# One-core decode attention beside a Mish layer: pack-by-pack loops with planned waits become loops over single batches with token semaphores

## The chip, the cores and the metric

The kernel runs on one core of one Trainium2 chip. The metric is the device time of one execution in microseconds (us); the kernel before takes 1303.63 us, the median of three runs (1303.53 to 1303.74). Engines are named as in the profile: PE (TensorE; PEld is its weight load), DVE (VectorE), ACT (ScalarE), POOL (GpSimd) and SP (SyncE, which issues the loads here).

## The reference

```python
xn = _layernorm(x, axis=-1)                                   # x: 8 x 1 x 512
q = (xn @ wq).reshape(8, 1, 32, 128).transpose(0, 2, 1, 3)    # 32 heads of 128
k = jnp.repeat(k_cache, 4, axis=1)                            # 8 kv heads, 8192 keys, 128
v = jnp.repeat(v_cache, 4, axis=1)
scores = jnp.einsum("bhqd,bhkd->bhqk", q, k) * (128 ** -0.5)
o = jnp.einsum("bhqk,bhkd->bhqd", _softmax(scores), v)
attention = o.transpose(0, 2, 1, 3).reshape(8, 1, 4096) @ wo
h = xn @ w1 + b1                                              # 512 -> 1792
mish = (h * jnp.tanh(softplus(h))) @ w2                       # 1792 -> 512
out = x + attention + mish
```

All is float32. The two caches hold 268 MB each; wq and wo 8.4 MB each, w1 and w2 3.67 MB each.

## The kernel before, in words

A **unit** is one batch with a pair of kv heads: 8.39 MB of keys and 8.39 MB of values, each one load of 64 KB per partition. There are 32 units. Two of them (batches 2k and 2k+1 of the same pair of heads) make a **pack**; 16 packs. Four packs make one pair of heads through all eight batches. wq and wo are loaded in four quarters each, one for each pair of heads.

Buffers: kvw holds a quarter of wq or wo; kva holds values; kvb holds keys and is a quarter larger than a unit, so that the next keys may overwrite the first three quarters of the old ones before the last quarter is read (plan_k; the products run forward in one unit and backward in the next).

For each unit, PE multiplies the keys with the queries (scores, tile c). The queries stand in qT, spread by a mask over 64 columns, so a product fills a 128x64 tile of the array, and two such tiles (two column halves) work side by side: 32 products, which PE runs as 64 passes. ACT copies c to sc, and PE sums it by the selection csel into the rows of S (rows, tile s), for both units of a pack.

For each pack, after its second unit: DVE takes the maximum over s, has it turned twice by PE (tiles nm, nr, nx, nmx), and makes the shifts nms (maximum). ACT takes exponents of s in two halves (exponents); DVE transposes each half from wide to raw, folds it, and adds the parts into the weights pt (fold, weights); the sums of the exponents go to l, ls, lsel (row_sums).

For each unit, PE then multiplies the values with pt (values, tile o): 32 products of 128x32 tiles, four side by side, 64 passes. **The values that a pack's loop multiplies are those of the pack before** (p - 1), so their weights are complete long ahead. DVE gathers o by quarters into os (gather), PE merges it (merge), DVE normalises it into oT (collect). After four packs oT is turned into oW (turn) and multiplied with a quarter of wo (outputs); DVE adds the result to acc.

Who waits for whom is worked out ahead of the build: class Program records every operation with the tiles it reads and writes, finds the conflicts, gives every pair of engines a semaphore and writes each wait at its instruction. PE, DVE and ACT run a hardware loop over packs 1 to 15; pack 0 and the end are written out. Each rare part (turn, queries, outputs) sits under a condition. The loads are in one queue on SP, in a planned order (plan, pump, release): each is issued when its buffer is free. With pack p's keys of unit b come the values of unit b of pack p - 1. The end of the queue loads w2 in three parts and the last quarter of wo in two, alternately; small products of w2 and wo then fill PE, after rounds of filler products (unread) that nobody reads.

All instructions of the kernel before carry line 383 (Program.issue) in the profile.

Of the kernel before, what the change touches and what calls it, by code (L numbers as in the profile page):

```python
# [8 lines left out]
AF = mybir.ActivationFunctionType  # L9
ALU = mybir.AluOpType  # L10
AX = mybir.AxisListType

P = 128
B = 8
# [23 lines left out]
PACKS = PAIRS * NP  # L38
R = P // G
# [5 lines left out]


KX = KR // 4

# [11 lines left out]
W2R = G * FT // 2 * FP // P  # L60
FAR = 1e38


ENGINES = ("tensor", "vector", "scalar", "gpsimd", "sync")
LOOPED = ("tensor", "vector", "scalar")
FIRST, END = 1, PACKS
RARE = ("w",)
SOMETIMES = {
    "turn": lambda p: (p + 27) & 19,
    "queries": lambda p: (p + 1) & 19,  # L70
    "outputs": lambda p: (p + 27) & 19,
}


class Op:
    def __init__(self, engine, method, make=None, outs=(), ins=(), stream=None, to=None):
        self.engine, self.method, self.make = engine, method, make
        self.outs, self.ins, self.to = outs, ins, to
        self.who = stream or engine
        self.unit = 16 if stream else 1  # L80
        self.waits = []


class Engine:
    def __init__(self, program, name):
        self.program, self.name = program, name

    def vary(self, method, make):

        args = make(self.program.pack)  # L90
        return self.add(method, args, {}, make)

    def __getattr__(self, method):
        return lambda *args, **kw: self.add(method, args, kw)

    def add(self, method, args, kw, make=None):
        more = {k: kw.pop(k) for k in ("stream", "to") if k in kw}
        after = kw.pop("after", ())
        outs = [kw["out"] if "out" in kw else args[0]]
        outs += [kw["accum_out"]] if "accum_out" in kw else []  # L100
        aps = [a for a in (*args, *kw.values()) if isinstance(a, bass.AP)]
        here = [a for a in aps if a.tensor.name in self.program.on_chip]
        ins = [a for a in here if not any(a is o for o in outs)]
        outs = [a for a in outs if a.tensor.name in self.program.on_chip]
        op = Op(self.name, method, make, outs, ins, **more)
        op.args, op.kw = args, kw
        return self.program.add(op, after)


class Program:  # L110

    def __init__(self, nc):
        self.nc = nc  # L120
        self.ops, self.count = [], {}
        self.know = {e: {} for e in ENGINES}
        self.seen = {}
        self.on_chip, self.psum = set(), set()
        self.pack, self.name, self.zone, self.at = None, None, "before", 0
        self.sends, self.numbers = {}, {}
        self.starts, self.sems, self.unit = {}, {}, {}

    def __getattr__(self, engine):
        if engine not in ENGINES:  # L130
            raise AttributeError(engine)
        return Engine(self, engine)

    def enter(self, pack):
        looped = pack in range(FIRST, END)
        if looped or self.zone == "loop":
            self.starts[pack] = len(self.ops)
        self.zone = "loop" if looped else "after" if self.starts else "before"
        self.pack, self.at, self.name = pack, 0, None

    def part(self, name):

        self.name = name
        self.at += 1

    def relay(self, engine, to, after):

        return self.add(Op(engine, "relay", to=to), [after])

    def settle(self, engine):  # L150

        last = [o for o in self.ops if o.who == engine][-1]
        self.add(Op(engine, "settle"), [last])

    @staticmethod
    def region(ap):
        (step, n), *free = ap.ap
        p, f = divmod(ap.offset, step)
        return p, p + n, f, f + 1 + sum(s * (c - 1) for s, c in free)

    def conflicts(self, op):

        found = {}
        for ap, writes in [(a, False) for a in op.ins] + [(a, True) for a in op.outs]:
            r = self.region(ap)
            for (who, wrote, q), o in self.seen.setdefault(ap.tensor.name, {}).items():
                if who == op.engine == "tensor":
                    continue
                hit = r[0] < q[1] and q[0] < r[1] and r[2] < q[3] and q[2] < r[3]
                hit = hit and (writes or wrote)  # L170
                if ap.tensor.name in self.psum and who != op.engine:
                    hit = all(
                        r[k] // n <= (q[k + 1] - 1) // n and q[k] // n <= (r[k + 1] - 1) // n
                        for k, n in ((0, 32), (2, 512))
                    )
                if hit and (who not in found or o.n > found[who].n):
                    found[who] = o
        return sorted(found.values(), key=lambda o: -len(o.clock))
# [1004 lines left out]
```

## Time and profile before

| | |
|---|---|
| median of the timed runs | 1303.63 us |
| the profiled execution, first to last instruction (its span) | 1302.2 us |
| busy: PE, DVE, ACT | 869.0, 389.9, 122.2 us |
| moved by the load queue | 561.06 MB |
| passes of keys x queries (tile c), without filler | 2048, in 32 units |
| passes of values x weights (tile o) | 2048, in 32 units |

The execution that was profiled took 1302.2 us from its first to its last instruction; the median of the timed runs lies 1.4 us above that. A row of the timeline has the start in us, the busy time in us, the engine, the line, the operation, the tiles as written<-read, shapes and count; in brackets stands the idle time of the engine ahead of it and what ended it. "64*128 64x512" is a product with 64 rows and 128 columns of weights and 512 columns streamed. A row of the waits has the total, the number of times and the longest.

### The profile page before, as it was taken

The page shows a single profiled execution, that of the slowest core. Times are in us where ns is not written, and L with a number is a line of the kernel's source. Part 1 is how long each engine was busy: PE and PEld are TensorE (multiplying, and loading weights), DVE is VectorE, ACT ScalarE, POOL GpSimd, SP SyncE. Part 2 cuts the span into 40 slices and gives each one's busy share as a digit, 9 for nine tenths or more (in the row PEclk, how much of TensorE's full clock was granted, in tenths as well). Part 3 has the DMA queues.
Part 4 walks back from the last instruction along what each step waited for, and adds up shares of the span by engine and source line. Part 5 has one row for each costly group of instructions (what it writes and reads, how often), then busy time and mean ns, then how long its engine had stood idle before and what let it go on. Part 6 is the DMA issues. An engine that isn't in the chain of part 4 may idle for free.

```text
span 1302.2 us, 11363 instructions
## 1 busy us (share of the span) xinstructions
PE 869.0 (67%) x4814; PEld 278.5 (21%) x4814; DVE 389.9 (30%) x597; ACT 122.2 (9%) x294; POOL 4.8 (0%) x10
## 2 busy tenths in 40 slices
PE   4786666766567665686656686666866656756568
PEld 1222112212112221122211222111221121212113
DVE  6350504305051230521405132052320515105061
ACT  1020202001020100200102020020100102001020
POOL 1000000000000000000000000000000000000000
PEclk9898789887799788897877897778877888878779
DMA  9999999999999999999999999999999999999998
GB/s 404 447 419 446 421 441 429 431 439 429 439 429 441 425 443 423 436 433 431 439 429 439 420 450 425 441 425 441 429 431 439 429 439 429 441 425 439 427 429 372
DMA packets 11554, 561.22 MB, mean 431 GB/s; under 512 B 1292, under 2 KB 1424, under 8 KB 1688
## 3 DMA queue, kind: packets, MB, share of 16 engines
q1 hardware_dynamic: 11520, 561.06, 99.7%
q8 instruction: 7, 0.11, 0.0%
q10 hardware_dynamic: 24, 0.02, 0.0%
q14 instruction: 3, 0.02, 0.0%
HBM read 561.01 MB, written 0.07 MB: 431 GB/s over the span
## 4 chain that ended last, share of the span: by engine, by line
DMA 61%; PE 31%; DVE 1%; issue 0%; SPq 0%; ACT 0%; DVEq 0%
DMA kvb<-in_kT 60%; PE c L383 29%; DMA kvb<-in_w 2%; PE o L383 1%; DVE raw L383 0%; DVE pt L383 0%; PE h L383 0%; DVE os L383 0%; DVE nm L383 0%; PE s L383 0%; PE m L383 0%; SPq L383 0%; ACT sc L383 0%; DVE acc L383 0%; DVE nr L383 0%
## 5 line engine op out<-in xcount | busy, mean ns | idle before, releaser
L383 PE MATMUL c<-kvb,qT 128*64 128x512 f32 x1984 | 497.7, 665 | 332.8 <-DMA kvb<-in_kT 332.2
L383 PEld LDWEIGHTS c<-kvb,qT 128*64 128x64 f32 x1984 | 160.8, 154 | 669.6 <-issue 459.4
L383 PE MATMUL o<-kva,pt 128*32 128x512 f32 x1984 | 238.0, 635 | 24.5 <-DMA kva<-in_v 24.1
L383 DVE TENSOR_REDUCE nm<-s 128x1 f32<-128x1024 f32 x16 | 19.6, 1225 | 437.0 <-PE s L383 437.0
L383 DVE STREAM_TRANSPOSE raw<-wide 128x2048 f32<-128x2048 f32 x36 | 125.5, 3485 | 19.5 <-ACT wide L383 17.7
L383 ACT COPY sc<-c 128x512 f32<-128x512 f32 x32 | 18.8, 586 | 979.1 <-PE c L383 979.1
L383 PEld LDWEIGHTS o<-kva,pt 128*32 128x32 f32 x1984 | 64.6, 116 | 189.1 <-issue 147.6
L383 ACT ACTIVATE wide<-s,nms 128x512 f32<-128x512 f32 x128 | 88.0, 688 | 130.4 <-DVE nms L383 66.9
L383 DVE TENSOR_TENSOR oT<-m,rt 128x16 f32 (+1 forms) x17 | 3.0, 175 | 229.6 <-PE m L383 229.6
L383 DVE TENSOR_SCALAR os<-o,isel 128x128 f32<-128x128 f32 x32 | 11.2, 350 | 151.1 <-PE o L383 151.1
L383 DVE TENSOR_TENSOR pt<-raw 64x256 f32<-64x256 f32 x128 | 53.6, 418 | 1.9
L383 DVE TENSOR_TENSOR qT<-qc,bsel 128x1024 f32<-128x1024 f32 x34 | 40.2, 1221 | 13.3 <-PE s L383 13.3
L383 PE MATMUL s<-sc,csel 64*128 64x512 f32 x128 | 37.1, 656 | 8.5 <-ACT sc L383 7.1
L383 DVE TENSOR_TENSOR raw<-raw 128x1024 f32<-128x1024 f32 x32 | 39.2, 1225 | 2.9 <-DVE raw L383 0.2
L383 DVE SCALAR_TENSOR_TENSOR os<-o,isel,os 128x128 f32<-128x128 f32 x96 | 33.6, 350 | 3.4
L383 ACT ACTIVATION_READ_ACCUMULATOR wide<-s,nms 128x1 f32 x128 | 24.7, 193 | 0.0
L383 PE MATMUL m<-hsel,os 128*128 128x8 f32 x66 | 12.7, 265 | 10.5 <-DVE lsel L383 10.5
L383 PE MATMUL m<-ident,nm 128*1 128x128 f32 x16 | 4.3, 270 | 21.6 <-DVE nm L383 21.6
L383 PE MATMUL h<-kvw,xnT 128*64 128x512 f32 x64 | 17.6, 700 | 0.0
L383 PE MATMUL c<-kva,qT 128*64 128x512 f32 x64 | 15.7, 652 | 2.1 <-DMA kva<-in_kT 2.1
L383 DVE TENSOR_SCALAR wide<-h 128x512 f32<-128x512 f32 x16 | 11.1, 691 | 19.9 <-PE h L383 19.5
L383 PEld LDWEIGHTS m<-hsel,os 128*128 128x128 f32 x66 | 10.1, 193 | 25.3 <-issue 12.2
(92 smaller groups left out, 162.1 us busy)
## 6 DMA issues: line engine op xcount, KB each, us to landing
kvw<-in_wq SPq DMA_DIRECT2D x4, 2048.0 KB, 30.3
kva<-in_v SPq DMA_DIRECT2D x2, 4096.0 KB, 21.6
kvw<-in_wo SPq DMA_DIRECT2D x3, 2048.0 KB, 30.4
kva<-in_v SPq DMA_DIRECT2D x1, 6144.0 KB, 24.3
kva<-in_w SPq DMA_DIRECT2D x1, 3584.0 KB, 15.8
kva<-in_v SPq DMA_DIRECT2D x1, 2048.0 KB, 28.8
kvb<-in_w SPq DMA_DIRECT2D x1, 2048.0 KB, 13.7
kvw<-in_wo SPq DMA_DIRECT2D x1, 1536.0 KB, 16.9
```

Source lines behind the costliest of these rows:

```text
L383: got = getattr(engine, o.method)(*args, **kw)
```

## The change

The planner (classes Op, Engine, Program) is removed. Each engine's program is now written out: PE loops over units n from -1 to 31, DVE and ACT over packs. Semaphores are tokens: whoever waits takes the token back by an instruction of its own (take), and DVE's own order is kept by a counter (class Chain).

- **Loads.** Keys of unit n, then values of unit n - 1 (before: of two units back). kvb is now one unit long, so keys n + 1 wait until the products with keys n are over (k_free); values n wait until the products with values n - 1 are over (v_free, passed on by DVE). The first load after wq is keys 0, then w1, then the second quarter of wq.
- **Key products.** qT is spread over 32 columns. Each product takes 64 of the 128 rows and 32 columns; 64 products in eight positions of the array, into two banks C[0] and C[1], which ACT copies both. The row products of both units (8 instead of 2 + 2) follow the second unit.
- **Values.** They are multiplied in the iteration of the next unit, after a token p_is of their own pack. DVE tells p_is after the sums of a pack (for its first unit), and once more after it has gathered the first unit and copied the second unit's weights, pt[:, 1], to pt[:, 0]. There is one tile o for both.
- **End.** The last values go to kvb (three quarters, one quarter), then wo's last quarter, whole, then w2 in four parts to kva. wo's products come ahead of w2's, with 512 columns; w2's first part is added in the same bank; the rest has 128 columns. Two rounds of filler stand between the last values and the merges (before: two rounds in each of three places).
- w1's products use four positions of 16 columns and are put in order by a product with shuf.

```diff
-        order = range(KR) if n % 2 == 0 else range(KR - 1, -1, -1)
-            for c in range(2):
-                last = pe.matmul(
-                    C[b][HE * c : HE * (c + 1), :],
-                    t[:, r],
-                    k[:, r * BW + c * 512 : r * BW + (c + 1) * 512],
...
+    def scores():
+        take(pe, s.k_in, 16)
+        take(pe, s.q_is)
+        take(pe, s.c_free)
+        t = qT.rearrange("p r u h -> p r (u h)")
+        for r in range(KR):
+            for c in range(2):
+                for e in range(2):
+                    g, rows = 2 * c + r % 2, slice(HE * e, HE * (e + 1))
+                    last = pe.matmul(
+                        C[e][Q * g : Q * (g + 1), :],
+                        t[rows, r],
+                        kvb[rows, r * BW + c * 512 : r * BW + (c + 1) * 512],
...
+    def later_loads():
+        load_wq(1)
+        for n in range(1, UNITS):
+            load_k(n)
+            p, b = divmod(n, PB)
+            if b == 0 and p in (1, 2):
+                load_wq(p + 1)
+            if b == 0 and p in (4, 8, 12):
+                load_wo(p // 4 - 1)
+            load_v(n - 1)
...
+        with pe.Fori(-1, UNITS) as n:
+            with part(pe, n & 32):
+                scores()
...
+            with part(pe, (n - 1) & 33):
+                rows()
+            with part(pe, (n - 3) & 33):
+                merges()
+            with part(pe, (n - 9) & 39):
+                turn()
+                outputs().then_inc(s.h_done, 1)
+            with part(pe, (n + 1) & 57):
+                queries()
+            with part(pe, (n - 1) & 32):
+                take(pe, s.v_in, 16)
+                take(pe, s.p_is)
+                values(kva).then_inc(s.valued, 1)
...
+            row_sums()
+            dve.tell(s.p_is)
...
+            dve.pass_on(s.valued, s.v_free)
+            gather(0)
+            dve.tensor_copy(pt[:, 0], pt[:, 1])
+            dve.tell(s.p_is)
```

PE, the loop of the kernel before, from its second unit's keys (c) to the values (o) of the pack before; the names in brackets are semaphores.

```order
L383 MATMUL c<-kvb,qT 64x512 [waits k_tensor]
L383 MATMUL c<-kvb,qT 64x512 x31
L383 MATMUL m<-hsel,os 128x8 [waits vector_tensor]
L383 MATMUL s<-sc,csel 128x512 [waits scalar_tensor]
L383 MATMUL s<-sc,csel 128x512
L383 MATMUL m<-ident,nm 1x128 [waits vector_tensor]
L383 MATMUL m<-ident,nx 128x1 [waits vector_tensor]
...
L383 MATMUL o<-kva,pt 32x512 [waits v_tensor]
L383 MATMUL o<-kva,pt 32x512 x31
```

PE, the same stretch of the changed kernel: an iteration of an odd unit.

```order
L437 MATMUL c<-kvb,qT 32x512 [waits k_in,q_is,c_free]
L437 MATMUL c<-kvb,qT 32x512 x63
...
L453 MATMUL s<-sc,csel 128x512 [waits c_free]
L453 MATMUL s<-sc,csel 128x512 x7
L462 MATMUL m<-ident,nm 1x128 [waits max_is]
L464 MATMUL m<-ident,nx 128x1 [waits max_wide]
...
L551 MATMUL x<-hsel,os 128x8 [waits o_is]
...
L528 MATMUL o<-kva,pt 32x512 [waits v_in,p_is]
L528 MATMUL o<-kva,pt 32x512 x31
```

The key products are twice as many with half the columns, the row products of the pack stand in one place, and the value products wait for p_is beside their load.

SP, the end of the queue of the kernel before, from the last two units' values on (kvb<-in_w and kvw<-in_wo are w2 and wo).

```order
L383 DMA kvb<-in_v 128x16384 [waits tensor_sync]
L383 DMA kva<-in_v 128x12288 [waits vector_sync]
L383 DMA kva<-in_v 128x4096
L383 DMA kvb<-in_w 128x4096 [waits vector_sync]
L383 DMA kvw<-in_wo 128x3072
L383 DMA kvb<-in_w 128x2560
L383 DMA kvw<-in_wo 128x1024
L383 DMA kvb<-in_w 128x512
```

SP, the same of the changed kernel, from the last keys on.

```order
L204 DMA kvb<-in_kT 128x16384 [waits k_free]
L204 DMA kva<-in_v 128x16384 [waits v_free]
L204 DMA kvb<-in_v 128x12288 [waits k_free]
L204 DMA kvb<-in_v 128x4096 [waits k_free]
L204 DMA kvw<-in_wo 128x4096 [waits w_free]
L204 DMA kva<-in_w 128x4096 [waits v_free]
L204 DMA kva<-in_w 128x1536 [waits v_free]
L204 DMA kva<-in_w 128x1024 [waits v_free]
L204 DMA kva<-in_w 128x512 [waits v_free]
```

wo's last quarter has moved whole ahead of w2, w2 goes to kva and waits there for the products with the last but one values, and one value load less follows the last keys.

More of the change, by code (lines that the diff above doesn't have):

```diff
@@ L60 @@
 W2R = G * FT // 2 * FP // P
+W2N = 2 * W2R
 FAR = 1e38
[L64 to L81, printed above, removed]
@@ L84 @@
[L84 to L91, printed above, removed]
-    def __getattr__(self, method):
[L94 to L107, printed above, removed]
@@ L698, in setup @@
[L698 to L712 removed]
+            M[:, : QR * B].rearrange("p (r o b) -> p r o b", r=QR, o=1).to_broadcast([P, QR, 2, B]),
+        )
@@ L787, in rows @@
[L787 to L803 removed]
+            qc[:, pair],
@@ L910, with merges @@
-    tid = wide[:, : OR * P].rearrange("p (r g i) -> p r g i", r=OR, g=G)
-    def turning():
-        dve.tensor_copy(
-            tid,
-            ident.rearrange("p (i r o) -> p r o i", r=OR, o=1).to_broadcast([P, OR, G, Q]),
-        )
-    def turn(last=False):
+                os[b], O[:, DH * i : DH * (i + 1)], isel[:, i : i + 1], os[b], op0=ALU.mult, op1=ALU.add
+            )
+    def merges():
+        take(pe, s.o_is)
+        for b in range(PB):
+            at = 168 + b * 2 * REP
+            pe.matmul(X[:, at : at + 2 * REP], os[b], hsel, start=True, stop=True)
+        pe.matmul(X[:, 136 : 136 + PB * 2 * REP], ones, lsel, start=True, stop=True).then_inc(s.merged, 1)
```

1163 lines of the change are left out of this document (475 added, 688 removed).

## The prediction

> **What bounds the kernel now.** I read the page's DMA rows first, then the list of waits, then the timeline of one pack in the middle.
>
> ```profile
> DMA  9999999999999999999999999999999999999998
> HBM read 561.01 MB, written 0.07 MB: 431 GB/s over the span
> q1 hardware_dynamic: 11520, 561.06, 99.7%
> DMA 61%; PE 31%; DVE 1%; issue 0%; SPq 0%; ACT 0%; DVEq 0%
> PE c L383 <- DMA kvb<-in_kT: 332.2, 30, 12.4
> ```
>
> The one queue of loads is busy for 99.7% of the span. PE waits 332.2 us for key loads, 30 times, and only the loads wait for nothing. So the kernel takes as long as its 561 MB take, plus what follows the last load. No engine's time matters, unless it makes a load start late.
>
> ```profile
> 313.65 15.58 PE L383 MATMUL c<-kvb,qT 128*64 128x512 f32 x64 [9.51 <-DMA kvb<-in_kT]
> 325.82 0.33 SPq L383 DMA_DIRECT2D kvb<-in_kT  x1
> 332.91 7.07 PE L383 MATMUL o<-kva,pt 128*32 128x512 f32 x64 [1.87 <-DMA kva<-in_v]
> 340.10 0.33 SPq L383 DMA_DIRECT2D kva<-in_v  x1
> 352.25 16.75 PE L383 MATMUL c<-kvb,qT 128*64 128x512 f32 x64 [12.28 <-DMA kvb<-in_kT]
> 373.31 7.07 PE L383 MATMUL o<-kva,pt 128*32 128x512 f32 x64
> 391.05 16.12 PE L383 MATMUL c<-kvb,qT 128*64 128x512 f32 x64 [10.67 <-DMA kvb<-in_kT]
> ```
>
> Key products start as their keys land: 313.65, 352.25, 391.05. Two 8.39 MB loads (one of keys, one of values) therefore take 38.7 us, 19.35 each. Each next load is issued well before the one in flight lands: keys at 325.82, values at 332.91, 7.1 us to spare; values at 340.10, keys at 352.25, 12.2 to spare. The value products never wait for their weights, which a whole pack earlier made.
>
> **The change, step by step.** The loads are the same 561 MB through the same queue, so every gain or loss is a gap in the queue or a longer tail. Key products: a unit's 64 passes on 2 tiles become 128 passes on 8. One pass of 512 columns takes 0.43 us (32 steps of two in 15.6 and 16.8; 16 steps of four in 7.07), so 8 tiles at once make 16 steps, like the value products. They start on an idle PE, which is slower at first, as a value run after 10 us of idling shows:
>
> ```profile
> 1228.16 15.70 PE L383 MATMUL c<-kvb,qT 128*64 128x512 f32 x64 [12.28 <-DMA kvb<-in_kT]
> 1243.92 0.59 ACT L383 COPY sc<-c 128x512 f32<-128x512 f32 x1 [37.51 <-PE c L383]
> 1244.56 1.13 PE L383 MATMUL s<-sc,csel 64*128 64x512 f32 x4 [0.37 <-ACT sc L383]
> 1245.76 1.22 DVE L383 TENSOR_REDUCE nm<-s 128x1 f32<-128x1024 f32 x1 [28.18 <-PE s L383]
> 1248.37 0.23 DVE L383 TENSOR_SCALAR nms<-far,nmx 128x4 f32<-128x4 f32 x1
> 1251.88 3.64 DVE L383 STREAM_TRANSPOSE raw<-wide 128x2048 f32<-128x2048 f32 x1 [0.95 <-ACT wide L383]
> 1255.62 0.69 ACT L383 ACTIVATE wide<-s,nms 128x512 f32<-128x512 f32 x1 [3.77 <-DVEq L380]
> 1258.64 0.19 ACT L383 ACTIVATION_READ_ACCUMULATOR wide<-s,nms 128x1 f32 x1
> 1257.13 0.35 DVE L383 TENSOR_SCALAR os<-o,isel 128x128 f32<-128x128 f32 x1 [0.23 <-PE o L383]
> 1257.52 1.12 DVE L383 SCALAR_TENSOR_TENSOR os<-o,isel,os 128x128 f32<-128x128 f32 x3
> 1260.38 3.60 DVE L383 STREAM_TRANSPOSE raw<-wide 128x2048 f32<-128x2048 f32 x1
> 1267.20 0.23 DVE L383 TENSOR_SCALAR lsel<-tsel,ls 128x16 f32<-128x16 f32 x1
> 1268.01 9.37 PE L383 MATMUL o<-kvb,pt 128*32 128x512 f32 x64
> ```
>
> The cold run of values took 9.37 us, the warm one 7.07; cold key products exceed 32 steps of 0.43 by 1.8 and 3.0 us. I take **9.2 us** for either run in the new order, where both follow long idling; 7.1 and 10 are the bounds.
>
> *The wait that is added.* The loads now alternate strictly: keys of 2p+1, values of 2p, keys of 2p+2, values of 2p+1. PE's products with values 2p need the weights of pack p (token p_is), and pack p's scores are complete only with keys 2p+1. Values 2p land 19.35 us later, the next keys 38.7 us later. The load of values 2p+1 needs kva, so it waits until the products with 2p end. Behind PE's waiting instruction stand the key products of 2p+2, whose keys land meanwhile; behind SP's waiting load stands the load of keys 2p+3. So if scores, softmax and values together take longer than 38.7 us, less what a load needs to start, the queue runs dry once a pack. The clock of one pack, from the first key product on:
>
> - key products: 9.2.
> - two copies by ACT instead of one (0.59 each, and 0.07 of waiting): 1.3.
> - the row products of both units at once: 8 instructions, 16 passes, two row halves side by side, so 8 steps. A step is 0.53 by the rows at 96.15 and 97.21 below (two steps between them): 4.3. At 0.43 a step it is 3.4; one at a time, 8.5.
>
> ```profile
> 37.66 15.33 PE L383 MATMUL c<-kvb,qT 128*64 128x512 f32 x64 [10.07 <-DMA kvb<-in_kT]
> 96.15 1.13 PE L383 MATMUL s<-sc,csel 64*128 64x512 f32 x4
> 97.21 7.07 PE L383 MATMUL o<-kva,pt 128*32 128x512 f32 x64
> 1291.10 1.10 PE L383 MATMUL m<-oT,wide 128*128 128x64 f32 x8 [0.27 <-DVE oT L383]
> 1292.14 1.93 PE L383 MATMUL h<-kvb,aT 128*8 128x128 f32 x64
> 1297.95 1.28 PE L383 MATMUL h<-kvb,aT 128*8 128x128 f32 x40 [1.59 <-DMA kvb<-in_w]
> 1300.30 0.29 DVE L383 COPY acc<-h 128x128 f32<-128x128 f32 x1 [7.50 <-PE h L383]
> 1300.62 0.35 SPq L383 DMA_DIRECT2D out<-acc  x1
> out<-acc SPq DMA_DIRECT2D x1, 64.0 KB, 1.5
> L383 DVE COPY wide<-ident 128x512 f32<-128x512 f32 x4 | 2.5, 614 | 0.0
> L383 DVE COPY oW<-m 32x64 f32<-32x64 f32 x14 | 3.1, 220 | 5.1 <-PE m L383 4.9
> ```
>
> - maximum and shifts, unchanged: 1245.69 (row products' end) to 1248.60, 2.9.
> - exponents, transposes, weights, sums: 1248.60 to 1258.83 as before (the last exponent's end). There the second transpose waited for the gather of values until 1260.38; the gather now stands elsewhere, so it starts at 1258.9 and its 7.05 us (1260.38 to 1267.43) end 17.35 after the shifts.
> - some ten waits are now instructions of their own. No row has their price; 0 to 2 us, I take 0.7, about the 0.07 that separates the copy from PE's end, ten times.
>
> Weights stand at 35.75. Values: 9.2, to 44.95. Relay by DVE and issue by SP: 0.15. A load that starts in an idle queue also pays its start: the 64 KB store landed 1.5 us after issue, 0.15 of that moves bytes at 431 GB/s, so 1.3. The lost time is 44.95 + 0.15 + 1.3 - 38.7 = **7.7 us per pack**. Fifteen packs have a second value load into kva, 15 x 7.7 = 115.5. In five of them 2 MB of wq or wo stand between the keys and the values (4.9 us at 431 GB/s each), which fill that much of the gap: minus 24.5. Three packs turn outputs ahead of the transposes, beyond the exponents' cover by some 0.3: 1. **Gaps: 92.**
>
> *Start.* wq, keys 0, w1, wq 1, keys 1 is the new order. Keys 0 land 8.5 us (w1's 3.67 MB) before the old 37.66, at 29; their products end at 38.4 and release keys 1 while wq 1 moves until 42. The Mish chain has keys 1's 19.4 us as cover. Cost 0; with 16 us products it would be 5.
>
> *Tail.* The queue has 52 us left after the last keys (two value loads, 13.4 us of wo and w2), so without gaps these products would start at 1228.16 + 19.36 = 1247.5, since the old order had one more value load behind them. From there: the weights are ready and values 30 end at 44.95; gather (1.6 with its wait, from the rows at 1257.13 and 1257.52) and the copy of the second half of the weights (1024 columns, 614 ns per 512: 1.2), 47.7; values 31, 7.9 between warm and cold, 55.6; gather 1.6, merges and normalising 1.1, turn 1.1 (the row above), four copies of 220 ns 0.9, 60.3; wo's 16 passes in 4 steps and w2's first 16 in another 4, 1.9 each, 64.1; the sum 0.7, the last small products 1.2, 66; copy and store 1.9 (1300.30 to 1302.2), 67.9. w2's own load waits for values 30 and lands at 55, so it hides. 1247.5 + 67.9 = 1315.4, **13 us** past the old end. The filler moved in this stretch hides in DVE's gather.
>
> Other edits have one answer, 0: half-size expansions of queries, the mask and identity set-up, loops and branches stand beside loads; if they came onto the chain, they would add 1 or 2 us per pack.
>
> Sum, from the profiled execution's own span: 1302.2 + 92 + 13 = 1407; the median of the timed runs lies 1.4 above that span, so **1409**.
>
> **The rivals.**
>
> *Tiles that only partly overlap.* Four tiles ran in full step here (64 passes, 16 steps in 7.07), and two row halves did (four passes, 1.06). Both at once no row shows. If eight tiles save half of what the step from 32 to 16 promises, key products take 24 steps: 24 x 0.43 + 2.1 of cold start = 12.4, 3.2 more per pack, 1409 + 16 x 3.2 = 1460. The Trainium skill's "TensorE: Matmul & The Clock Gate", Measured speedup vs the span model, has speedups of 6.32 for nine tiles and 10.6 for sixteen, about two thirds of the count, which would put eight at some 5.4 tiles, the same 24 steps; by that rule the sum is 1460, and the trace agrees with it in no row, since four tiles reach all of four here.
>
> *Row halves don't overlap within a column.* Then 32 steps, as now, 16.05 us: 6.85 more per pack, 110, plus 5 at the start: 1524. Against: the row products' 1.06 us; and 64 passes of 128 columns issue in 1.93 us (0.03 each), so issue is no limit.
>
> *A shorter chain.* Both runs warm (7.07), row products 3.4, waits free: 5.9 less, a gap of 1.8 in ten packs and none in five, and a tail of 7: 1302.2 + 19 + 7 + 1.4 = 1330.
>
> *The other side: the wait doesn't bind.* If PE's first value products of a pack found a token left over, they would start when values 2p land, 19.35 after the keys, and end at 28; kva would be free 9 us before keys 2p+2 land, the queue would stay full, and w2 would land last, as now: 1304, no change. What decides is whether these products wait for anything of their own pack. (Weights ready by 28, 37.4 less 9.2, would close the gaps too, but leave some of the tail.) Against: tokens are told twice and taken twice a pack, and the first is told after the pack's own sums. That is also the case in which the change doesn't do what it says.
>
> **How the numbers follow.** Forecast 0.74, partial tiles 0.09, no row overlap 0.08, shorter chain 0.06, no wait 0.03. The forecast's own range is a gap of 5 to 10 us: 1368 to 1444, and a few us of tail either way. To hold eight in ten I reach past the partial tiles above and toward the short chain below: 1350 to 1475; the 1524 and 1304 cases, and 1330, are left out. Slower by more than 0.2% (2.6 us; about what a measurement of this kernel tells from none) is all but the last rival: 0.97; within, 0.02; faster, 0.01.
>
> **What would show it.** In the changed profile: SP's second value load of a pack issued some 45 us after that pack's second key products start, and the queue's busy share near 92%, not 99.7; GB/s near 400. Key products in about 9 us, with eight pass starts together; 15 to 17 would be the no-overlap rival, 12 the partial one. PE's wait for pt about 17 us per pack, a row that the old profile lacks. If value loads are still issued before keys land, the whole argument falls; if the gaps are there but shorter than 5 us, a term of the clock is too long, and the row products are the first to look at.

## The result and the profile after

The changed kernel takes **1428.67 us**, the median of four runs (1427.9 to 1430.61), beside 1303.66 for the kernel before, measured along with it: 1.0961 times as long, 95% interval 1.0945 to 1.0976. The profiled execution spans 1427.0 us, 124.8 more than the 1302.2 of before.

On the page of the changed kernel, the busy share of the DMA engines over 40 slices, the load queue, the bytes, and the two costliest groups on PE:

```profile
DMA  9899999899997998989999798998999799898994
q1 hardware_dynamic: 11376, 561.06, 91.8%
HBM read 561.01 MB, written 0.07 MB: 393 GB/s over the span
L528 PE MATMUL o<-kva,pt 128*32 128x512 f32 x1984 | 269.4, 704 | 455.9 <-PEq L98 455.9
L437 PE MATMUL c<-kvb,qT 64*32 64x512 f32 x4096 | 261.6, 664 | 187.0 <-PEq L98 187.0
```

The same two groups in the kernel before:

```profile
L383 PE MATMUL c<-kvb,qT 128*64 128x512 f32 x1984 | 497.7, 665 | 332.8 <-DMA kvb<-in_kT 332.2
L383 PE MATMUL o<-kva,pt 128*32 128x512 f32 x1984 | 238.0, 635 | 24.5 <-DMA kva<-in_v 24.1
```

The bytes are the same; the queue is no longer full (91.8% instead of 99.7). PE's work on keys has about halved (261.6 us; before 497.7 and another 15.7 for the unit in kva), and the kernel is slower all the same. A wait that is an instruction of its own shows as PE's sequencer (PEq L98, the helper take). 455.9 us of it stand ahead of the value products, which before waited 24.5.

One pack in the middle. PE, with ACT's copies and SP's next load into kva:

```profile
666.88 9.09 PE L437 MATMUL c<-kvb,qT 64*32 64x512 f32 x128 [10.89 <-PEq L98]
676.34 1.07 ACT L727 COPY sc<-c 128x512 f32<-128x512 f32 x2 [41.47 <-ACTq L98]
677.46 3.70 PE L453 MATMUL s<-sc,csel 64*128 64x512 f32 x16 [1.50 <-ACT sc L727]
701.78 8.69 PE L528 MATMUL o<-kva,pt 128*32 128x512 f32 x64 [16.34 <-PEq L98]
710.41 7.10 PE L437 MATMUL c<-kvb,qT 64*32 64x512 f32 x128
710.59 0.33 SPq L204 DMA_DIRECT2D kva<-in_v  x1
732.86 8.52 PE L528 MATMUL o<-kva,pt 128*32 128x512 f32 x64 [15.36 <-PEq L98]
752.28 9.06 PE L437 MATMUL c<-kvb,qT 64*32 64x512 f32 x128 [10.90 <-PEq L98]
```

DVE in the same pack, from the shifts to the last row of the sums (the second transpose and the folds left out):

```profile
684.33 0.23 DVE L72 TENSOR_SCALAR nms<-far,nmx 128x4 f32<-128x4 f32 x1
687.62 3.60 DVE L72 STREAM_TRANSPOSE raw<-wide 128x2048 f32<-128x2048 f32 x1 [1.31 <-DVEq L98]
701.35 0.23 DVE L72 TENSOR_SCALAR lsel<-tsel,ls 128x16 f32<-128x16 f32 x1
```

Read as one loop: keys 2p+1 land at 666.88; 34.9 us later the weights stand and the products with values 2p begin; they end at 710.5, and only then is the next load into kva issued, at 710.59, 43.7 after the keys. It lands at 732.86, 22.3 later; the keys behind it land 19.4 later, at 752.28. 43.7 + 22.3 + 19.4 = 85.4 us per pack, against 77.4 for four loads in a full queue. That is 8.0 too much. Between 666.88 and 752.28 the queue also carried 2 MB of wo. A pack without them takes 85.4 too (581.5 to 666.9); they move in the time in which the queue is empty, so five packs lose only 3.1.

From the start of unit 1's key products to that of unit 31's the changed kernel takes 1289.8 us. Ten packs of 77.4 (four loads of 19.35) and five of 82.3 (with 2 MB of wq or wo, 4.9) would be 1185.5, so **104.3 us** are lost in packs. Three of them, those that turn outputs, take 88.2 to 88.4 instead of 85.4. The first of these, from PE's turn to the first transpose:

```profile
427.43 1.94 PE L569 MATMUL x<-oT,tid 128*128 128x64 f32 x8 [1.47 <-PEq L98]
429.52 0.97 DVE L72 COPY oW<-x 32x64 f32<-32x64 f32 x4 [2.63 <-DVEq L98]
430.86 3.62 DVE L72 STREAM_TRANSPOSE raw<-wide 128x2048 f32<-128x2048 f32 x1 [0.37 <-DVEq L98]
```

The transpose starts at 430.86, though ACT's last exponent of that half ends at 427.94 (427.27 and 0.67 long): DVE waits for the turn and copies it first.

The start: first queries and first key products on PE, and SP's load of keys 1:

```profile
22.89 5.10 PE L390 MATMUL h<-kvw,xnT 128*64 128x512 f32 x16 [8.06 <-PEq L98]
34.80 9.39 PE L437 MATMUL c<-kvb,qT 64*32 64x512 f32 x128 [6.81 <-PEq L98]
44.34 0.33 SPq L204 DMA_DIRECT2D kvb<-in_kT  x1
```

The queries start at 22.89, not at 13.98 as before. Keys 1 are issued at 44.34, when the queue has been empty since 42.1. From unit 1's key products on (66.6) a full queue would need 1185.5 us to the 1247.5 at which the prediction put the last ones, so they would stand at 62.0: the start costs **4.6 us**.

The end, from the last values to the products with wo and w2:

```profile
1402.88 7.08 PE L528 MATMUL o<-kvb,pt 128*32 128x512 f32 x64 [2.90 <-PEq L98]
1416.42 3.60 PE L596 MATMUL h<-kvw,oW 128*8 128x512 f32 x16 [1.48 <-PEq L98]
1419.79 2.95 PE L676 MATMUL h<-kva,aT 128*8 128x512 f32 x16
```

Keys 31 are multiplied from 1356.5 on, and the span ends 70.5 us later. 70.5 less the 54.7 of loads and finish that a full queue would leave (1302.2 less 1247.5) makes a tail of **15.8 us**. 4.6 + 104.3 + 15.8 = 124.7, the whole difference of 124.8 but for rounding.

### The profile page after: what moved, and what is told of

Same layout as the page of the kernel before. It is cut to its first block, busy times and chain, and to the rows that moved or that the text cites. A ratio compares the mean times of both kernels' runs of the same rounds, so it can differ in the third digit from the quotient of the medians.

```text
span 1427.0 us, 16576 instructions
## 1 busy us (share of the span) xinstructions
PE 678.1 (48%) x6824; PEld 222.2 (16%) x6824; DVE 386.2 (27%) x614; ACT 146.2 (10%) x339; POOL 4.9 (0%) x10
## 3 DMA queue, kind: packets, MB, share of 16 engines
q1 hardware_dynamic: 11376, 561.06, 91.8%
## 5 line engine op out<-in xcount | busy, mean ns | idle before, releaser
L528 PE MATMUL o<-kva,pt 128*32 128x512 f32 x1984 | 269.4, 704 | 455.9 <-PEq L98 455.9
L437 PE MATMUL c<-kvb,qT 64*32 64x512 f32 x4096 | 261.6, 664 | 187.0 <-PEq L98 187.0
L528 PEld LDWEIGHTS o<-kva,pt 128*32 128x32 f32 x1984 | 74.6, 127 | 645.8 <-issue 645.8
L437 PEld LDWEIGHTS c<-kvb,qT 64*32 64x32 f32 x4096 | 82.0, 118 | 365.3 <-issue 365.3
L727 ACT COPY sc<-c 128x512 f32<-128x512 f32 x64 | 34.4, 589 | 646.8 <-ACTq L98 646.6
L453 PE MATMUL s<-sc,csel 64*128 64x512 f32 x256 | 59.3, 602 | 24.0 <-ACT sc L727 24.0
L72 DVE TENSOR_TENSOR qT<-qc,bsel 128x512 f32<-128x512 f32 x33 | 22.9, 693 | 77.1 <-DVEq L98 74.9
L453 PEld LDWEIGHTS s<-sc,csel 64*128 64x128 f32 x256 | 23.4, 186 | 61.1 <-ACT sc L727 38.5
L596 PE MATMUL h<-kvw,oW 128*8 128x512 f32 x64 | 14.4, 1049 | 5.9 <-PEq L98 5.9
L551 PE MATMUL x<-hsel,os 128*128 128x8 f32 x64 | 10.7, 275 | 5.1 <-PEq L98 5.1
## 6 DMA issues: line engine op xcount, KB each, us to landing
kvw<-in_wo SPq DMA_DIRECT2D x4, 2048.0 KB, 33.5
```

The source lines that it names most:

```text
L72: got = getattr(self.e, method)(*args, **kw)
L437: last = pe.matmul(C[e][Q * g : Q * (g + 1), :], t[rows, r], kvb[rows, r * BW + c * 512 : r * BW + (c + 1) * 512], start=(r < 2), stop=(r ...
L453: last = pe.matmul(S[:, c * 512 : (c + 1) * 512], csel[half_of, b, e].rearrange("p u b h -> p (u b h)"), sc[b][e][half_of, :], start=(b == ...
L528: last = pe.matmul(O[Q * c : Q * (c + 1), :], pt[:, b, j % 2, j // 2].rearrange("p t e h -> p (t e h)"), vt[:, W4 * DH * j : W4 * DH * (j ...
L551: pe.matmul(X[:, at : at + 2 * REP], os[b], hsel, start=True, stop=True)
L596: last = pe.matmul(H[Q * r : Q * r + B, :], oW[:, r, h, :], kvw[:, at : at + D], start=(h == 0), stop=(stop and h == 1))
```

## The experiments

Ratios are to the kernel before, with 95% intervals; the changed kernel's is 1.0961. "Left of the packs" means the part of the 104.3 us that remains, from the same two starts. The diffs show the main lines of each edit.

**No wait for the pack's own weights** (e1_const). The even units' value products take a mask that stands from the start, so the even units' attention is left out; the odd units still wait for p_is.

```diff
-                    pt[:, b, j % 2, j // 2].rearrange("p t e h -> p (t e h)"),
+                    pt[:, b, j % 2, j // 2].rearrange("p t e h -> p (t e h)") if own else rsel,
...
-            dve.tell(s.p_is)
...
-            with part(pe, (n - 1) & 32):
+            with part(pe, (n - 1) & 33):
+                take(pe, s.v_in, 16)
+                values(kva, own=False).then_inc(s.valued, 1)
+            pe.end_ifs()
+            with part(pe, (n - 2) & 33):
```

> The products with the even units' values take a constant mask (rsel) in place of the weights pt, and no longer wait for p_is; all else stays, so the results of the even units' attention are left out. Theory (values of a pack's first unit wait for that pack's softmax, kva stays taken, and the queue runs dry): these products start when their load lands, about 19 us after the key products, and the 104 us that lie between the key products of the fifteen packs go; 1427 - 104 and a few us of the tail, 1315 to 1330 us. Rival (the transfers themselves are slower in the new order: the load queue is busy 91.8%, some packets take 3 us): 1400 to 1430. Rival (PE is slower, colder, in the new tile shape): 1400 to 1430.

Measured: 1348.02 us (1342.78 to 1351.09), ratio 1.0347 (1.033 to 1.0364). Of the 104.3 us in packs 26.6 are left. The forecast of this run was too low, because one thing still waits. PE, and SP's next load into kva:

```profile
557.10 9.22 PE L437 MATMUL c<-kvb,qT 64*32 64x512 f32 x128 [10.75 <-PEq L98]
576.40 9.80 PE L528 MATMUL o<-kva,rsel 128*32 128x512 f32 x64 [0.78 <-PEq L98]
592.65 0.33 SPq L204 DMA_DIRECT2D kva<-in_v  x1
```

The products start as their values land, 19.3 after the keys, and end at 586.2. But DVE passes the buffer's token on, and DVE does so behind its softmax, at 592.6. So the load is issued 35.6 us after the keys instead of 43.7, not the 29 that PE allows. In this pack that is just in time (it takes 78.0 us). In others DVE comes later: in the pack whose keys start at 233.53 the load is issued 40.9 us after them, the queue stands empty from 271.31 to 275.38, and the pack loses 5.0, the most of all. The wait for p_is was the greater part of the loss; the place of DVE's relay behind the softmax keeps a part.

**Value loads by quarters** (e2_quarters). The wait stays; each quarter of kva is released and loaded by itself, so that the first is issued before the products end.

```diff
+        for i in range(PARTS):
+            cols = slice(i * PW, (i + 1) * PW)
+            load(v_ins[i], kva[:, cols], unit(v, n)[:, cols], s.v_free, PARTS * (n - 1) + i + 2 if n else 1)
...
+                for i in range(PARTS):
+                    take(pe, v_ins[i], 16)
+                    at = ROUNDS * i // PARTS
+                    values(kva, at, at + ROUNDS // PARTS).then_inc(s.valued if i == PARTS - 1 else s.read, 1)
```

> Each value load is split into four loads of a quarter, each with its own landing; PE tells after each quarter of the products, and each quarter of kva is released by itself. The wait for the weights stays. Theory (the gap is the end of the value products in kva, 43.6 us after the key products): the first quarter comes free 6.5 us sooner, the ten full gaps of 8 us shrink to 1 to 2, the five that hold weights (3 us) vanish: 65 to 85 us less, 1343 to 1365 us. Rival (slow transfers): four times as many loads, no gain, 1420 to 1450. Rival (the weights alone, not the products behind them, set the gap): no gain either.

Measured: 1375.27 us (1373.25 to 1379.3), ratio 1.0548 (1.0524 to 1.0572). 50.6 us are left of the packs. In the pack whose keys start at 647.98:

```profile
683.94 9.07 PE L533 MATMUL o<-kva,pt 128*32 128x512 f32 x64 [16.85 <-PEq L98]
687.69 5.77 SPq L204 DMA_DIRECT2D kva<-in_v  x4
```

The weights are as late as ever (36.0), but the first quarter is issued 39.7 us after the keys instead of 43.7. With the wait untouched and the release earlier, half of the loss goes, so it is a matter of when kva is free, as the prediction had it. The run is still 10 us above the range that I expected. The 39.7, with 2.9 for the restart of the queue (worked out below), are still 3.9 more than the 38.7 that two loads give, and full packs that don't turn outputs lose 2.1 to 5.4.

**One row half after the other** (e3_halves). The key products keep their number; the loop over the row halves stands outside, so that four positions of the array work at a time, not eight.

```diff
-        for r in range(KR):
-            for c in range(2):
-                for e in range(2):
+        for e in range(2):
+            for r in range(KR):
+                for c in range(2):
```

> The key products run over all of one row half first, then the other: the same 128 passes, but only four positions of the array are in use at a time. Theory: eight positions do run at once in the changed kernel (9.1 us), so here the products take 16, 7 us longer, and all of it is on the path: 15 x 7 and 4 at the start, 1527 to 1550 us. Rival (PE is not on the path): within 5 us of 1429. Rival (the row halves don't run at once now): no change of the products' 9.1 us.

Measured: 1638.23 us (two runs, 1632.22 and 1644.24), ratio 1.2565 (1.2512 to 1.2618); the profiled span is 1642.6. One pack on PE:

```profile
669.92 19.68 PE L437 MATMUL c<-kvb,qT 64*32 64x512 f32 x128 [10.55 <-PEq L98]
717.11 9.72 PE L528 MATMUL o<-kva,pt 128*32 128x512 f32 x64 [16.09 <-PEq L98]
768.59 19.84 PE L437 MATMUL c<-kvb,qT 64*32 64x512 f32 x128 [10.41 <-PEq L98]
```

The pack takes 98.7 us, 13.3 more than 85.4: 10.6 of key products, 1.7 of row products (5.40 instead of 3.70, in the trace), 1.0 of values. Sixteen times 13.3 is 213, and the run is 210 longer. So the key products lie on the path one for one, and eight positions did work at once in the changed kernel. I had expected 7 us a pack. At full clock four positions alone cost 5.2: in the even units, behind value products, the key products take 12.27 (at 726.77) instead of 7.10. The rest is time at half clock, in the row and value products too. Busy time by stretches in this run, with the granted clock in the column ahead of the last two:

```profile
670.00:675.00 5.00, 5.00 (x24) 1.21 (x28) 0.00 (x0) 0.00 (x0) 0.00 (x0) 0.50 0.97 419
...
680.00:684.00 4.00, 4.00 (x40) 1.12 (x36) 0.00 (x0) 0.00 (x0) 0.00 (x0) 0.50 1.21 524
...
686.00:690.00 4.00, 3.60 (x36) 0.82 (x28) 0.00 (x0) 0.07 (x1) 0.00 (x0) 1.00 0.08 33
```

The same view of the changed kernel, whose products start at 666.88:

```profile
669.00:671.00 2.00, 2.00 (x24) 0.51 (x16) 0.00 (x0) 0.00 (x0) 0.00 (x0) 0.51 1.21 524
671.00:673.00 2.00, 2.00 (x48) 0.74 (x40) 0.00 (x0) 0.00 (x0) 0.00 (x0) 1.00 0.62 262
```

With eight positions at work PE gets its full clock 3.6 to 4.7 us after its products start, in all seventeen runs of key products that start cold. With four it comes 12.1 to 15.4 us after, in the seventeen of this run, although PE is busy all the time. It comes within 3.5 us after the products have passed to the second row half (11.9 after the start), so this run doesn't tell whether the number of positions counts or the row half.

**Values two units behind keys again** (e4_lag). The value products stand between the row products and the merges, DVE's gather moves with them, and the last values and w2 lie in the buffers of before; loops, tokens and tiles stay as changed.

```diff
-            load_v(n - 1)
+            if n > 1:
+                load_v(n - 2)
...
+            with part(pe, (n - 2) & 32):
+                take(pe, s.v_in, 16)
+                take(pe, s.p_is)
+                values(kva).then_inc(s.valued, 1)
```

> The values lag two units behind the keys again, as in the kernel before, and are multiplied between the pack's row products and the merges; the last but one values go to kvb, the last and w2 as before. Eight positions, tokens, loops, the order at the start and wo ahead of w2 stay. Theory: loads are issued 10 us and more ahead, no gap in the packs; what stays is 4.7 us at the start and a tail longer than before's by 5 to 10 us: 1309 to 1320 us. Rival (tokens, loops or tile shape cost the time): above 1400. Rival (slow transfers of the new order and buffers): 1360 to 1400.

Measured: 1352.96 us (1350.25 to 1353.44), ratio 1.037 (1.0353 to 1.0387). PE in the middle:

```profile
560.11 9.14 PE L439 MATMUL c<-kvb,qT 64*32 64x512 f32 x128 [10.86 <-PEq L98]
598.82 8.56 PE L439 MATMUL c<-kvb,qT 64*32 64x512 f32 x128 [6.78 <-PEq L98]
637.58 9.65 PE L439 MATMUL c<-kvb,qT 64*32 64x512 f32 x128 [10.38 <-PEq L98]
```

38.7 us from keys to keys, as in the kernel before, with loops, tokens, small tiles and moved fillers all in place. After 200 us the queue never empties before the end. So values one unit behind keys, with the places of products and gather that go with it, cost what the packs lost from there on. I had expected 1309 to 1320. What I missed is before 200 us and at the end. The queue stands empty for 5.5, 11.0, 5.5 and 11.1 us, ending at 47.4, 78.9, 104.9 and 199.6: first at the start, as in the changed kernel; then because keys 2 follow keys 1 in one buffer with no value load between; and twice because a load of wq that waits for DVE stands in SP's queue ahead of a value load. At the end DVE in this order gathers the values before ahead of the pack's transposes, and from unit 31's key products on the run takes 85.4 us, where the kernel before takes 74.0 with the same loads behind them.

**Turning behind the softmax** (e5_late), in the changed kernel.

```diff
-            with part(e, (p - 4) & 19):
-                keep_turned()
-                dve.close()
-            e.end_ifs()
...
-            with part(e, (p - 4) & 19):
-                add_outputs()
-                dve.close()
-            e.end_ifs()
...
+            with part(e, (p - 4) & 19):
+                keep_turned()
+                add_outputs()
+                dve.close()
+            e.end_ifs()
```

On DVE both parts now stand behind the gather of the pack's first values; PE's turn and output products move behind the value products of that iteration.

> Only the turning of outputs moves: DVE's waits and copies for it stand behind the pack's softmax, and PE's turn and output products behind the value products. Theory: in the three packs that turn outputs the first transpose waited for the turning, 3.0 us more than the 0.3 that I had put down, so these packs (gaps of 10.8 to 11.1) fall to the 8.0 of the others: 1428.7 less 8 to 9, 1419 to 1421. Rival one, it is the added work itself and not its place: no change, 1427 to 1430. Rival two, the turning behind the value products delays the next key products instead: slower, 1430 or more.

Measured: 1415.72 us (1415.52 to 1416.18), ratio 1.0859 (1.0841 to 1.0878): 13.0 less, more than expected. The three packs now take 85.4 each, so 9 us are the turning. Another 1.6 is at the start: unit 1's keys are multiplied at 65.0 instead of 66.6, in a part of the program that this edit doesn't touch. The other packs take 1.5 less together, and what is left lies between the profiled executions and the medians. PE in the first of the three packs:

```profile
452.39 1.08 PE L569 MATMUL x<-oT,tid 128*128 128x64 f32 x8 [3.18 <-PEq L98]
458.48 8.25 PE L437 MATMUL c<-kvb,qT 64*32 64x512 f32 x128
```

The even unit's key products now start 52.8 us after the odd unit's (405.65), in the changed kernel 46.6, and nothing waits for that: they still end before the value load that restarts the queue has landed (471.5).

**First queries ahead of the loop** (e6_start).

```diff
         turn_x()
-        with pe.Fori(-1, UNITS) as n:
+        queries()
+        with pe.Fori(0, UNITS) as n:
```

> Only the first queries on PE move: they stand ahead of the loop over units, which now begins at unit 0. Theory: the 4.7 us at the start come from PE's taken branch over the loop's parts, 6.35 us long, whose instructions arrive behind the loads; without it the first queries start near 14 instead of 22.9, keys 1 are issued while w1 is still in flight, and the all-idle gap of the queue at 42.1 goes: 1428.7 less 3 to 4.7, 1424 to 1426. Rival, the landing of wq or of keys 0 ends that wait anyway: 1427 to 1430 and the first queries stay near 23.

Measured: 1424.43 us (1423.41 to 1425.86), ratio 1.0924 (1.0906 to 1.0942), 4.2 less, as expected.

```profile
14.27 6.46 PE L390 MATMUL h<-kvw,xnT 128*64 128x512 f32 x16
28.29 9.70 PE L437 MATMUL c<-kvb,qT 64*32 64x512 f32 x128 [7.56 <-PEq L98]
```

The first keys are multiplied 6.5 us earlier, and the gap at 42.1 is gone. In the changed kernel PE passed over the empty parts of iteration -1 first; the trace has one taken branch of 6.35 us there, in which a 16 KB packet of instructions arrived between the loads' 64 KB packets. That the branch waited for that packet is read from their times, not shown apart.

**Quarters, with both moves** (e7_joined): the edits of e2, e5 and e6 together.

> Value loads by quarters, together with the two moves of the other runs (turning behind the softmax, first queries ahead of the loop). Theory: the mended losses add up: 1375.3 less 3 times 3.5 to 4.7 for the turning and 3 to 4.7 for the start, 1357 to 1363; what is left above 1303.7 is then the tail (13.5) and the packs' staggered quarters. Rival, the losses overlap (a gap mended in one pack comes back as the next one's wait): 1366 to 1375.

Measured: 1370.13 us (1366.27 to 1370.52), ratio 1.05 (1.0483 to 1.0518). The theory expected 1357 to 1363 and was wrong; the rival has it. The start gave its 4, but the three turning packs take 83.1 to 83.2 instead of 83.4 to 83.9. One of them, whose odd keys start at 396.02:

```profile
449.73 7.10 PE L442 MATMUL c<-kvb,qT 64*32 64x512 f32 x128
456.97 0.33 SPq L204 DMA_DIRECT2D kvb<-in_kT  x1
```

The moved turn and output products delay the even unit's key products, which end 61 us after the odd keys, so the next key load is issued when the queue is nearly or wholly dry (empty at 456.85). In e5 that delay was covered by a longer gap; here the gap is short and the cover gone. A gain measured in one order isn't a term that can be added in another.

**Three orders mended** (e8_order): values two units behind, the first values loaded ahead of keys 2, wq 3 loaded one unit later, first queries ahead of the loop, DVE's first transposes ahead of the gather and its part of the turning behind the sums.

```diff
-            if b == 0 and p in (1, 2):
-                load_wq(p + 1)
+            if n == 1:
+                load_v(0)
+            if n in (2, 5):
+                load_wq(2 + n // 5)
...
-            load_v(n - 1)
+            if n > 2:
+                load_v(n - 2)
...
+            turn_exponents(0)
+            weights(0, 1)
+            dve.close()
             with part(e, (p - 1) & 16):
                 dve.pass_on(s.valued, s.v_free)
...
-            turn_exponents(0)
-            weights(0, 0)
-            weights(0, 1)
```

> Values two units behind keys, and three orders besides: the first value load before keys 2 and the loads of wq 2 and 3 behind key loads whose products release nothing they need; first queries ahead of the loop; on DVE the first half of the transposes ahead of the gather of the values before. Theory: with the wait out of the packs, what was left of that version (1353.0) is loads that queue behind loads that wait, at the start (33 us of gaps with the queue idle), and 9 us of DVE's order in the last pack; with some 5 to 9 us of gap left at the start and a tail 3 to 5 over the kernel before: 1312 to 1322. Rival, the rest lies in the loops with tokens themselves (branches, one wait an instruction): 1340 to 1353, with the queue idle in ordinary units too.

Measured: 1321.0 us (1320.21 to 1321.52), ratio 1.0131 (1.0114 to 1.0148). It doesn't beat the kernel before, but 107.7 of the 125 us are gone with the loops kept. The one gap left in the packs, 6.2 us with the queue empty, is where two key loads follow each other into one buffer:

```profile
101.30 9.81 PE L441 MATMUL c<-kvb,qT 64*32 64x512 f32 x128 [13.97 <-PEq L98]
111.26 0.33 SPq L204 DMA_DIRECT2D kvb<-in_kT  x1
133.36 9.14 PE L441 MATMUL c<-kvb,qT 64*32 64x512 f32 x128 [15.25 <-PEq L98]
```

Keys 3 land 7.8 us later than the load of wq and their own 19.4 would make it (101.30 + 4.9 + 19.4 = 125.6); the stretch between the last load and the store is 5.2 us longer than before (7.4 instead of 2.1), and some 4 us are scattered over the packs.

**PE kept busy ahead of the two runs on the chain** (e9_warm), in the changed kernel.

```diff
+            with part(pe, (n - 1) & 33):
+                pe.wait_ge(s.c_free, 1)
+                fill(11)
+            pe.end_ifs()
             with part(pe, n & 32):
                 scores()
...
+            with part(pe, (n - 1) & 33):
+                fill(14)
+            pe.end_ifs()
             with part(pe, (n - 1) & 32):
                 take(pe, s.v_in, 16)
```

> Added work only: before the key products of each odd unit PE runs 11 rounds of filler products, and before the value products of each even unit 14, so that it doesn't stand idle for 10.9 and 16.4 us ahead of the two runs on the pack's chain. Theory: these runs are long for the clock alone, so key products fall from 9.06 to 7.1 us and value products from 8.69 to 7.1; 3.6 us off each of ten packs with a gap of 8.0, about 3.0 off the five with a gap of 3, 3.6 off the tail: 1428.7 less 51 to 55, 1373 to 1378. Rival one, the filler is paid for with the clock granted elsewhere (the mean falls and other runs slow): 1390 to 1429. Rival two, the filler is itself too long and pushes the key or value products back: above 1429.

Measured: 1387.67 us (1386.67 to 1391.77), ratio 1.0641 (1.0623 to 1.0659): 41 less where 51 to 55 were expected.

```profile
656.42 7.10 PE L437 MATMUL c<-kvb,qT 64*32 64x512 f32 x128 [0.91 <-PEq L98]
689.39 7.07 PE L528 MATMUL o<-kva,pt 128*32 128x512 f32 x64 [1.30 <-PEq L98]
```

Where the filler fits, both runs are as short as expected, and four of the ten packs without wq or wo fall to 81.7 to 82.0. The granted clock didn't suffer; its mean rose from 0.750 to 0.876. What is missing is my filler: in four packs it ended 2.6 to 3.2 us ahead of the weights and the values took 8.5 to 8.8 after all. In the three turning packs it stood behind the output products and no pause is left between it and the value products, so these fell only to 85.5. The theory holds; its sum didn't.

**Filler at the end** (e10_tail), in the changed kernel.

```diff
         merges()
+        fill(1)
         turn()
+        fill(2)
         outputs(stop=False)
```

> Added work only: filler after the last merges (one round) and after the last turn (two rounds), ahead of the output products. Theory: the two runs of 16 passes with wo and w2 take 3.60 and 2.95 us instead of 1.9 because PE waits for DVE twice ahead of them and loses its clock; kept busy they take 1.9 each: 1428.7 less 2 to 2.7, 1426 to 1427. Rival, these products are long for their shape (128 rows by 8 columns) and not for the clock: still 3.6 and 2.9, and 1429 to 1430.

Measured: 1425.67 us (1424.5 to 1426.83), ratio 1.0938 (1.092 to 1.0956).

```profile
1415.27 1.90 PE L596 MATMUL h<-kvw,oW 128*8 128x512 f32 x16
1416.99 1.90 PE L676 MATMUL h<-kva,aT 128*8 128x512 f32 x16
```

Both are 1.90 now. From unit 31's key products to the end of the span there are 68.25 us instead of 70.55: 2.3 less, within the 2 to 2.7 expected. The medians differ by 3.0; the other 0.7 lies outside the filled stretch.

## Why the prediction was right, and where its sizes were off

The mechanism is the one predicted: PE's products with values 2p wait for the weights of their own pack, kva is free too late, and the queue runs dry once a pack. e1 takes the wait away, e2 its consequence, e4 the order that makes it; they take back 81, 53 and 76 of the 125 us. Each is less than I had expected of it, and what stays is found elsewhere in their traces. With the start and DVE's order mended too (e8), 107.7 come back; of the 17.4 left, the last 4 are not placed. The named rivals fell: 7.10 us for 128 passes are 16 steps and a half (neither partial tiles nor 32 steps), and the queue's share came to 91.8%, near the 92 that I had named.

The clock of one pack, by its own steps (predicted, then measured at 666.88):

| | predicted | measured |
|---|---|---|
| key products | 9.2 | 9.1 |
| copies and the wait behind them | 1.3 | 1.5 |
| row products | 4.3 | 3.7 |
| maximum and shifts | 2.9 | 3.4 |
| exponents to sums | 17.35 | 17.0 |
| waits as instructions, unplaced | 0.7 | 0.2 |
| value products | 9.2 | 8.7 |
| relay and issue | 0.15 | 0.1 |
| restart of the empty queue | 1.3 | 2.9 |
| the gap, of 85.4 less 77.4 | 7.7 | 8.0 |

The chain was put 1.4 too long and the restart 1.6 too short, and these nearly cancel; that the gap came out within 0.3 is in part luck. The restart of 2.9 is 22.3 from issue to landing (710.59 to 732.86) less the 19.4 of a load in flow (732.86 to 752.28). My 1.3 came from the 64 KB store. Of this load's 2.9, 0.96 lie between its issue and its first packet, and 0.7 between the end of its last packet (732.19) and the products. Its first packets are slow as well: on fifteen of the sixteen engines they take 2.6 to 3.4 us instead of 2.42. The remainder isn't placed. The Trainium skill's "DMA: Bandwidth & Descriptors", Anatomy of one DMA — SWDGE (gpsimd) path, has some 2.0 us as the fixed part of a transfer that GpSimd issues; this one is issued by SP, and the 2.9 measured here is above that.

For the rival with partial tiles my estimate from the Trainium skill's "TensorE: Matmul & The Clock Gate", Measured speedup vs the span model, was some 5.4 for eight tiles. The row at 710.41 decides against it for this shape: 128 passes in 7.10 us are eight positions of 64 by 32 at full rate.

The forecast lay 19.7 us low, in four sizes:

- **Packs that turn outputs**, put at 0.3 each beyond the others: 3.0. I had counted the turning as beside the exponents, but it starts only when the merge and the normalising are through, and PE turns at half clock (1.94 instead of 1.1). Three packs, 8.1 us; e5 takes these back.
- **The start**, put at 0: 4.6. I looked at loads and at products, not at how PE gets to its first product. e6 takes 4.2 back.
- **The gap**, 0.3 in each of fifteen packs: 4.5.
- **The tail**, put at 13: 15.8. The output products were taken at 1.9 each, from a row on a warm PE; here they run at half clock, 3.60 and 2.95. e10 shows it.

8.1 + 4.6 + 4.5 + 2.8 = 20. What stays open is what in PE's branches at the start takes the time: it differs by up to 3.6 us (first keys at 32.8 in e10, 33.5 in e5, 34.8 changed, 35.7 in e9, 36.4 in e4) with edits that don't touch it.

## What to carry to other kernels

In a kernel that is bound by one queue of loads, ask of each buffer what ends last before it is free, and lay the sum of that chain beside the time that the queue has in flight; halving an engine's work doesn't help if the same edit makes a buffer wait for a softmax. (It didn't hurt either: with that wait in place the long key products of e3 cost another 210 us.) Keeping the consumer one unit further behind cost no memory here, and in e4 the packs behind the start lost nothing any more. Shortening pieces of the chain (quarters, filler) gave back a part each, and the one sum of gains that was tried (e7) did not come out. When an engine idles in the middle of such a chain, take the durations of its next run from a row that follows a like idling, at the tail too.

## What the runs showed of the hardware

- How long PE stays at half clock depends on the positions of the array that work (how many or which, e3 doesn't tell): 3.6 to 4.7 us of products with eight positions of 64 by 32, 12.1 to 15.4 with four (granted 0.50 from 670 to 684 in e3, PE busy throughout). Once full, the clock stays so with four: in e3's even units all key products run at 1.00.
- How long PE idles doesn't decide alone whether it loses its full clock. In e2 it idles 2.96 to 2.98 us ahead of the last quarter's products thirteen times. Six times the clock stays and they take 1.92 us; seven times it falls and they take 2.5 to 3.4:

```profile
711.55 3.34 PE L533 MATMUL o<-kva,pt 128*32 128x512 f32 x16 [2.97 <-PEq L98]
955.94 1.92 PE L533 MATMUL o<-kva,pt 128*32 128x512 f32 x16 [2.97 <-PEq L98]
```

- In the traces the granted clock changes only on a grid of 3.41 us: in the changed kernel at 670.96, 684.62 and 705.10, four and six steps apart. In e2 it fell where 2.2 us or more of the idling lay between two lines of the grid, and stayed where a line cut it into parts of 2.0 or less. It fits the 8.77 us of value products in e9 after 2.64 of idling (605.90; 2.2 of them in one step) beside the 7.08 after 2.90 at the end of the changed kernel (1402.88; cut into 1.4 and 1.5). This is read from the traces; no run was made to test it.
- A thinly used PE loses its clock as well: at the end of the changed kernel it went from 1.00 to 0.50 ahead of the output products, though its longest wait there was 1.48 us.
- Filler products, 370 us of them, did not lower the clock granted to the rest (mean 0.876 in e9, 0.750 without).
